# Whole-float32 units of a decayed-attention kernel: heads in pairs, states kept in a PSUM bank, a two-slot pool for the rest

## The chip, the cores and the metric

The kernel runs on one core of a Trainium2 chip. The metric is the device time of one execution in microseconds (us), the median over runs of the kernel. The core has five engines that run side by side and meet at semaphores: TensorE (PE; its weight loads are listed apart as PEld), VectorE (DVE), ScalarE (ACT), GpSimd (POOL) and SyncE (SP), which here only starts transfers.

## What is computed

A decayed linear attention over 4 batches, 8 heads, 768 steps and a head width of 64, in float32, and behind it a two-layer network with a softplus, whose weights come as float64:

```python
def _attn_ref(q, k, v):
    ...
    for t in range(S):
        state = gamma[None, :, None, None] * state + np.einsum('bhd,bhe->bhde', k[:, :, t], v[:, :, t])
        y[:, :, t] = scale * np.einsum('bhd,bhde->bhe', q[:, :, t], state)
    return y.astype(np.float32)

def _moe_ref(x, w_in, w_out):        # w_in 512x2048, w_out 2048x512
    h = x @ w_in
    g = np.maximum(h, 0.0) + np.log1p(np.exp(-np.abs(h)))
    return (g @ w_out).astype(np.float32)
```

Here x is the attention's output with the heads side by side: 3072 tokens of 512 values.

## The kernel before

**Units.** The sequence is cut into chunks of 128 steps. A unit is one chunk of one batch and one half (`hf`) of the heads, four heads: 4 batches x 6 chunks x 2 halves, 48 units; unit 2c + hf is chunk c of batch 0. The decay is folded into q and v by two tables on POOL (L134, L135), so that the state is a plain sum of k-by-v products. The steps of a unit are functions that the table `PARTS` places on ticks, four ticks to a unit: `load_unit`, `decay`, `operands` (PE transposes k and q two heads at a time into `tp`, ACT and DVE copy them out), `scores` (k by q into `sc`, copied to `ah`, the upper triangle cut away by POOL), `new_state` (k by v into `pp`), and `stack_and_outputs` (the chunk's output `yp` from the scores and the state of the chunk before, L255 to L266; then the next state `st`, L231 to L241).

**Two kinds of units.** The first 12 units (`WHOLE`, batch 0) feed float32 operands to PE. An fp32 product stands in the trace as two matmul records, two passes. The 36 others split every operand into a high and a low part of type float32r, each a product of one pass, and sum three products.

**A whole unit before.** A head's scores are taken with both heads' k of a pair as weights (`kw`, 128 columns) and the head's q between zeros (`qw`). States and outputs go head by head, with 64 weight columns: four `pp` products (L208), added by DVE into `td` in SBUF (L216, L219), copied to `st` by ACT (L231, L232), and an output of 64 partitions for each head, from state and q (L255) and from v and scores (L261). ACT and DVE write the output's high and low parts into the ring `xh`, `xl` in two pieces each (L270, L272).

**A split unit before.** Per head one product of the high k with v's high and low part side by side (L212, 64 columns of weights, 128 moving) and one of the low k with v's high part (L213, 64 by 64); two additions on DVE (L219, L221); then `st` as high and low part (L237 to L241).

**The network** (called FFN below) goes block by block over the tokens (`BLOCKS`: two of 256, six of 384, one of 256). A step has `hidden` (into `hp`, L300 to L302, 256 or 384 columns moving), a softplus over DVE, ACT and POOL (L307 to L316) and `second` (into `acc`, L331 to L333, 512 columns). Its weights come in 16 slices `f`. `convert_weights` turns the float64 bits of a slice into a high and a low float32r part: ACT L84 and L90, DVE L92 to L94, ACT L96 (high part), POOL L97 (low part), through one PSUM buffer `wp`. A slice's load waits until the slice three before it has been converted (`FETCH`). Slices 0 to 9 are first used by block 0, 10 to 15 by block 1.

**Order.** A scheduler sets each engine's order from the code's order and from dependencies; each engine then runs its list in order. PSUM has eight banks: two for `hp`, three for `acc` and `wp`, and three slots of pool `ps_a`, taken in turn by `tp`, `sc`, `pp` and `yp`; a new tile waits until the tile three allocations back has been read.

## Time and profile before

| | before |
|---|---|
| three timed runs | 698.87, 698.94, 699.02 us |
| median | 698.94 us |
| the profiled execution's span | 699.0 us |
| busy: PE, DVE, ACT, POOL | 683.4, 444.5, 366.1, 284.0 us |
| read from HBM, written | 35.66 MB, 6.29 MB |

The span runs from the first to the last instruction of one profiled execution; it is as long as the slowest of the timed runs to the digit shown, so nothing has to be added for what lies around it. Busy time of PE counts overlapping matmuls once. A matmul's own duration is longer than what it costs in a row of them, because they are pipelined: its cost is the distance from its start to the start of the next.

### The profile page before, as it was taken

The page shows a single profiled execution, that of the slowest core. Times are in us where ns is not written, and L with a number is a line of the kernel's source. Part 1 is how long each engine was busy: PE and PEld are TensorE (multiplying, and loading weights), DVE is VectorE, ACT ScalarE, POOL GpSimd, SP SyncE. Part 2 cuts the span into 40 slices and gives each one's busy share as a digit, 9 for nine tenths or more (in the row PEclk, how much of TensorE's full clock was granted, in tenths as well). Part 3 has the DMA queues.
Part 4 walks back from the last instruction along what each step waited for, and adds up shares of the span by engine and source line. Part 5 has one row for each costly group of instructions (what it writes and reads, how often), then busy time and mean ns, then how long its engine had stood idle before and what let it go on. Part 6 is the DMA issues. An engine that isn't in the chain of part 4 may idle for free.

```text
span 699.0 us, 12543 instructions
## 1 busy us (share of the span) xinstructions
PE 683.4 (98%) x4480; PEld 618.7 (89%) x4480; DVE 444.5 (64%) x940; ACT 366.1 (52%) x854; POOL 284.0 (41%) x346
## 2 busy tenths in 40 slices
PE   6699999999999999999999999999999999999997
PEld 5588888999999999999999999999999999999996
DVE  4786777576757776566776676567667666533321
ACT  4886776464555546455554654455565444433221
POOL 5675577443333433433343333334334332322221
PEclk9999999999999999999999999999999999999999
DMA  9975751221111121111211112111211101000100
GB/s 257 248 199 177 197 174 24 46 68 40 46 38 24 31 69 38 31 23 39 69 31 23 38 37 63 38 23 32 68 38 24 31 16 61 1 1 0 46 1 31
DMA packets 90750, 42.77 MB, mean 61 GB/s; under 512 B 77376, under 2 KB 85568, under 8 KB 90688
## 3 DMA queue, kind: packets, MB, share of 16 engines
q1 hardware_dynamic: 90240, 41.96, 22.1%
q8 instruction: 36, 0.59, 0.4%
q14 instruction: 26, 0.21, 0.1%
q10 hardware_dynamic: 448, 0.01, 0.0%
HBM read 35.66 MB, written 6.29 MB: 60 GB/s over the span
## 4 chain that ended last, share of the span: by engine, by line
PE 87%; DMA 1%; DVE 0%; ACT 0%; issue 0%
PE acc L331 13%; PE hp L300 12%; PE acc L333 12%; PE acc L332 12%; PE hp L302 12%; PE hp L301 12%; PE sc L188 2%; PE pp L212 1%; PE yp L266 1%; PE yp L264 1%; PE yp L265 1%; PE tp L142 1%; PE tp L144 1%; PE yp L258 1%; PE yp L257 1%; DMA win<-in_moe_w_in_dram 1%
## 5 line engine op out<-in xcount | busy, mean ns | idle before, releaser
L316 POOL TENSOR_TENSOR gl<-sp,gh 128x384 fp32r<-128x384 f32 (+1 forms) x120 | 130.1, 1084 | 201.6 <-ACT gh L314 151.0
L300 PE MATMUL hp<-xh,winhl 128*128 128x384 f32 (+1 forms) x576 | 186.5, 324 | 0.3 <-DVE sp L312 0.3
L302 PE MATMUL hp<-xh,winhl 128*128 128x384 f32 (+1 forms) x576 | 183.8, 319 | 0.0
L301 PE MATMUL hp<-xl,winhl 128*128 128x384 f32 (+1 forms) x576 | 183.6, 319 | 0.0
L331 PE MATMUL acc<-wouthl,gh 128*128 128x512 f32 x384 | 155.5, 405 | 0.0
L332 PE MATMUL acc<-wouthl,gh 128*128 128x512 f32 x384 | 150.7, 393 | 0.0
L333 PE MATMUL acc<-wouthl,gl 128*128 128x512 f32 x384 | 150.4, 394 | 0.0
L307 DVE TENSOR_SCALAR sp<-hp 128x384 uint32<-128x384 uint32 (+1 forms) x120 | 69.7, 582 | 98.0 <-PE hp L302 93.7
L308 ACT ACTIVATE sp<-sp 128x384 f32<-128x384 f32 (+1 forms) x120 | 65.6, 546 | 97.7 <-DVE sp L307 97.3
L300 PEld LDWEIGHTS hp<-xh,winhl 128*128 128x128 f32 x576 | 108.8, 189 | 4.9 <-issue 0.5
L301 PEld LDWEIGHTS hp<-xl,winhl 128*128 128x128 f32 x576 | 108.9, 189 | 3.6 <-DVE xl L272 0.2
L302 PEld LDWEIGHTS hp<-xh,winhl 128*128 128x128 f32 x576 | 108.7, 189 | 0.9 <-issue 0.5
L314 ACT CAST gh<-sp 128x384 fp32r<-128x384 f32 (+1 forms) x120 | 64.0, 534 | 78.7 <-DVE sp L312 44.4
L312 DVE SCALAR_TENSOR_TENSOR sp<-hp,sp 128x384 f32<-128x384 f32 (+1 forms) x120 | 69.5, 579 | 25.7 <-ACT sp L308 24.8
L333 PEld LDWEIGHTS acc<-wouthl,gl 128*128 128x128 f32 x384 | 71.9, 188 | 15.4 <-issue 0.2
L331 PEld LDWEIGHTS acc<-wouthl,gh 128*128 128x128 f32 x384 | 72.2, 188 | 11.2 <-issue 0.3
L332 PEld LDWEIGHTS acc<-wouthl,gh 128*128 128x128 f32 x384 | 72.4, 189 | 10.2
L159 DVE TENSOR_TENSOR kq<-tp,kq 64x256 fp32r<-64x256 f32 x72 | 30.4, 422 | 68.6 <-ACT kq L157 67.5
L134 POOL TENSOR_TENSOR qn<-qn,qtabs 128x256 f32<-128x256 f32 x48 | 29.4, 613 | 105.5 <-DMA qn<-in_q_dram 80.5
L156 ACT CAST kq<-tp 64x512 fp32r<-64x512 f32 x72 | 41.8, 581 | 29.4 <-PE tp L144 27.8
L135 POOL TENSOR_TENSOR vn<-vn,vtabs 128x256 f32<-128x256 f32 x48 | 29.4, 613 | 48.5 <-DVE al L191 18.5
L272 DVE TENSOR_TENSOR xl<-yp,xh 64x256 fp32r<-64x256 f32 x96 | 39.9, 416 | 5.5 <-ACT xh L270 4.2
(85 smaller groups left out, 1088.4 us busy)
## 6 DMA issues: line engine op xcount, KB each, us to landing
win<-in_moe_w_in_dram SPq DMA_DIRECT2D x16, 512.0 KB, 4.1
wout<-in_moe_w_out_dram SPq DMA_DIRECT2D x16, 512.0 KB, 4.1
kn<-in_k_dram SPq DMA_DIRECT2D x48, 128.0 KB, 2.4
qn<-in_q_dram SPq DMA_DIRECT2D x48, 128.0 KB, 2.7
vn<-in_v_dram SPq DMA_DIRECT2D x48, 128.0 KB, 2.3
out_dram<-o SPq DMA_DIRECT2D x24, 256.0 KB, 2.1
gtab_sb<-in_gtab_dram ACTq DMA_DIRECT2D x2, 2.0 KB, 3.3
qtabs<-in_qtab_dram ACTq DMA_DIRECT2D x1, 4.0 KB, 2.3
```

The source lines that it names most:

```text
L156: nc.scalar.copy(kq[own, :2, par], tp[own])
L300: nc.tensor.matmul(hp[:, k], lhsT=wt[:, 0, d, :], rhs=xh[:, d, :], start=d == 0, stop=False)
L301: nc.tensor.matmul(hp[:, k], lhsT=wt[:, 0, d, :], rhs=xl[:, d, :], start=False, stop=False)
L302: nc.tensor.matmul(hp[:, k], lhsT=wt[:, 1, d, :], rhs=xh[:, d, :], start=False, stop=d == ND - 1)
L307: nc.vector.tensor_scalar(sp.bitcast(U32), hps[s].bitcast(U32), 0x80000000, None, op0=ALU.bitwise_or)
L308: nc.scalar.activation(sp, sp, AF.Softplus)
L312: nc.vector.scalar_tensor_tensor(g, hps.pop(s), 0.0, g, op0=ALU.max, op1=ALU.add)
L314: nc.scalar.copy(gh, g)
L316: nc.gpsimd.tensor_tensor(gl, sps.pop(s), gh.bitcast(F32), op=ALU.subtract)
L331: nc.tensor.matmul(acc[i][t], lhsT=gh[:, k, ts], rhs=wt[:, 0], start=begins and k == 0, stop=False)
L332: nc.tensor.matmul(acc[i][t], lhsT=gh[:, k, ts], rhs=wt[:, 1], start=False, stop=False)
L333: nc.tensor.matmul(acc[i][t], lhsT=gl[:, k, ts], rhs=wt[:, 0], start=False, stop=ends and f == fs[-1])
```

## The change

The last unit kinds, numbers and names stay; lines move down by 10 or so (L300 becomes L310, L331 becomes L341).

- **States in PSUM.** A bank of its own, `stp`, holds the sums for both halves, two head pairs each. A product takes both heads' k of a pair as weights (128 columns) and both heads' v as moving columns (128). Of the 128x128 result the two 64x64 diagonal blocks are the states; the other two blocks hold mixed products that are never read. The sums run on over a batch's chunks, and the first product of a batch clears the bank. `td` and its additions are gone. A split unit's state takes six products (three for each pair) where it took eight, a whole unit's two where it took four.
- **Pool.** `ps_a` has two slots instead of three.
- **Whole units.** k stands between zeros (`kz`), q as it is (`qs`). The state sits in `stw`, zero off the diagonal blocks, v between zeros (`vns`, three buffers that also take the split units' v). An output is 128 partitions for a pair: one product from the state and two from the scores, each with 128 weight columns. ACT and DVE write `xh` and `xl` in one piece of 128 partitions.
- **Split units** copy the state from PSUM in two ACT copies and two DVE subtractions (`od` is gone); their scores and outputs are as before.
- **Setup.** DVE clears the zero halves of `vns` and `stw`, POOL those of `kz`.

How the rows of the engines' lists move, at three places. First PE, around the scores of unit 3, where the FFN begins; before (names: `st_231` is the state of half 1, `sc`, `pp`, `tp`, `yp` the PSUM tiles of the steps above):

```order
L180 MATMUL sc<-qw,kw 128x128 x4
L208 MATMUL pp<-vn,kn 64x64 x4
L300 MATMUL hp<-xh,winhl 128x256 x2
L142 MATMUL tp<-ident,kn 128x128 x2
L144 MATMUL tp<-ident,qn 128x128 x2
L255 MATMUL yp<-qw,st_231 64x128
L301 MATMUL hp<-xl,winhl 128x256
```

and of the change:

```order
L310 MATMUL hp<-xh,winhl 128x256
L187 MATMUL sc<-qs,kz 128x128 x4
L311 MATMUL hp<-xl,winhl 128x256
L312 MATMUL hp<-xh,winhl 128x256
L225 MATMUL stp<-vn_89,kn 128x128 x2
```

The state's four 64x64 products became two of 128x128, and a first matmul of the FFN now stands ahead of unit 3's scores.

Second ACT, in the rows that lead up to the copies of unit 3's transposes (`tp_278` before, `tp_262` in the change), on which those scores wait; before (`winhl_394` and `wp_398` belong to slice 2, `win_268` is slice 3 as loaded):

```order
L96 CAST wouthl_334<-w_330 128x512
L84 ACTIVATE win_268<-win_268 128x512
L96 CAST winhl_394<-w_390 128x512
L90 ACTIVATE wp_398<-wout_203 128x512
L148 COPY kw_283<-tp_278 128x256
L149 COPY qw_83<-tp_278 64x256
```

and of the change (`winhl_360` is slice 2):

```order
L97 CAST wouthl_311<-w_307 128x512
L157 COPY kz_85<-tp_262 64x256
L264 CAST xh_81<-yp_270 128x2x128
L85 ACTIVATE win_256<-win_256 128x512
L159 COPY qs_86<-tp_262 128x256
L241 COPY stw0_87<-stp_92 64x2x64
L97 CAST winhl_360<-w_356 128x512
```

Slice 2's cast and the `wp` row stood ahead of the unit's copies; now they stand behind them.

Third PE, at the state of a split unit in the middle of the program; before (four such pairs of rows follow each other, two are shown, `acc_2126` is a result of the FFN's block):

```order
L332 MATMUL acc_2126<-wouthl,gh 128x512
L333 MATMUL acc_2126<-wouthl,gl 128x512
L212 MATMUL pp<-vhl,kh 64x128
L213 MATMUL pp<-vhl,kl 64x64
L212 MATMUL pp<-vhl,kh 64x128
```

and of the change, for a later unit:

```order
L312 MATMUL hp<-xh,winhl 128x384
L225 MATMUL stp<-vhl,kh 128x128 x2
L225 MATMUL stp<-vhl,kl 128x128
L195 MATMUL sc<-kq_83 128x256 x2
L225 MATMUL stp<-vhl,kh 128x128 x2
```

Eight products with 64 weight columns became six with 128.

The diff (in the split branch of `outputs`, and in the old copies to the ring, lines that only change their place are left out):

```diff
--- before.py
+++ after.py
@@ -49,7 +49,8 @@
     ffn = ctx.enter_context(tc.tile_pool(name="ffn", bufs=2))
     ps_h = ctx.enter_context(tc.tile_pool(name="ps_h", bufs=2, space=bass.MemoryType.PSUM))
     ps_o = ctx.enter_context(tc.tile_pool(name="ps_o", bufs=1, space=bass.MemoryType.PSUM))
-    ps_a = ctx.enter_context(tc.tile_pool(name="ps_a", bufs=3, space=bass.MemoryType.PSUM))
+    ps_a = ctx.enter_context(tc.tile_pool(name="ps_a", bufs=2, space=bass.MemoryType.PSUM))
+    ps_s = ctx.enter_context(tc.tile_pool(name="ps_s", bufs=1, space=bass.MemoryType.PSUM))
 
     nc.scalar.preload_act_table_set("softplus")
 
@@ -114,7 +115,16 @@
 
     kqs = [attn.tile([P, 3, 2, NJ, C], F32R, name=f"kq{i}") for i in range(2)]
 
-    qws = [attn.tile([P, 2, NJ, C], F32, name="qw", tag="vhl", bufs=2) for i in range(2)]
+
+
+    kz = attn.tile([P, 2, NJ, C], F32, name="kz", tag="vhl", bufs=2)
+    qs = attn.tile([P, 2, NJ, C], F32, name="qs", tag="vhl", bufs=2)
+    stw = [attn.tile([P, NJ, P], F32, name=f"stw{hf}", tag=f"st{hf}") for hf in range(2)]
+    vns = [attn.tile([P, HH, 2, D], F32, name=f"vn{i}") for i in range(3)]
+
+
+    stp = ps_s.tile([P, 2, NJ, P], F32, name="stp")
+    sides = ((0, lo, up), (1, up, lo))
 
     def load_unit(n):
         if n in loads:
@@ -122,7 +132,7 @@
         b, c, hf = units[n]
         tiles = []
         for nm, src in (("kn", k), ("qn", q), ("vn", v)):
-            t = attn.tile([P, HH, D], F32, name=nm, bufs=3 if nm == "vn" else 2)
+            t = vns[n % 3][:, :, 0, :] if nm == "vn" else attn.tile([P, HH, D], F32, name=nm, bufs=2)
             nc.sync.dma_start(t, src[b, hf * HH:(hf + 1) * HH, c * C:(c + 1) * C, :].rearrange("h s d -> s h d"))
             tiles.append(t)
         loads[n] = tiles
@@ -143,15 +153,13 @@
         for j in range(NJ):
             nc.tensor.transpose(tp[:, 1, j, :], qn[:, 2 * j:2 * j + 2, :], ident)
         if n < WHOLE:
-            kw = attn.tile([P, NJ, C], F32, name="kw", tag="kh")
-            qw = qws[n % 2]
-            nc.scalar.copy(kw, tp[:, 0])
-            nc.scalar.copy(qw[lo, 0], tp[lo, 1])
-            nc.vector.tensor_copy(qw[up, 1], tp[up, 1])
-            live[n] = [(kw, qw), kn, vn]
+            qt = qs[:, n % 2]
+            nc.scalar.copy(kz[lo, 0], tp[lo, 0])
+            nc.vector.tensor_copy(kz[up, 1], tp[up, 0])
+            nc.scalar.copy(qt, tp[:, 1])
+            live[n] = [qt, kn, vn]
             return
         kq = kqs[n % 2]
-        sides = ((0, lo, up), (1, up, lo))
         for par, own, oth in sides:
             nc.scalar.copy(kq[own, :2, par], tp[own])
             nc.scalar.copy(kq[oth, 1, par], tp[own, 1])
@@ -173,11 +181,10 @@
     def scores(n):
         kq = live[n][0]
         if n < WHOLE:
-            kw, qw = kq
             parts = [attn.tile([P, HH, C], F32, name="ah")]
             sc = ps_a.tile([P, HH, C], F32, name="sc", tag="a")
             for h in range(HH):
-                nc.tensor.matmul(sc[:, h, :], lhsT=kw[:, h // 2, :], rhs=qw[:, h % 2, h // 2, :], start=True, stop=True)
+                nc.tensor.matmul(sc[:, h, :], lhsT=kz[:, h % 2, h // 2, :], rhs=kq[:, h // 2, :], start=True, stop=True)
             nc.scalar.copy(parts[0], sc)
         else:
             parts = [attn.tile([P, HH, C], F32R, name=nm) for nm in ("ah", "al")]
@@ -196,80 +203,83 @@
             )
         live[n] += parts
 
+    began = {}
+
     def new_state(n):
         b, c, hf = units[n]
-        live[n].append(state[hf][0] if c else None)
+        live[n].append(state[hf] if c else None)
         if c == NC - 1:
             return
-        pp = ps_a.tile([D, HH, 2, D], F32, name="pp", tag="a")
+        for j in range(NJ):
+            hs = slice(2 * j, 2 * j + 2)
+            if n < WHOLE:
+                kn, vn = live[n][1:3]
+                products = [(kn, vn)]
+            else:
+                vhl, kh, kl = live[n][1:4]
+                vh, vl = (vhl[:, :, t, :] for t in range(2))
+                products = [(kh, vh), (kh, vl), (kl, vh)]
+            for i, (kk, vv) in enumerate(products):
+
+                first = c == 0 and hf == 0 and j == 0 and i == 0
+                m = nc.tensor.matmul(
+                    stp[:, hf, j, :], lhsT=kk[:, hs, :], rhs=vv[:, hs, :], start=first, stop=True, skip_group_check=True
+                )
+                if first:
+                    began[b] = m.ins
+                elif c == 0:
+                    tc.add_manual_dep(m.ins, began[b].name, mybir.DependencyInfo(mybir.DependencyClass.NoSync, mybir.DependencyReason.DATA), reason="the bank's first")
+
+    def stack_state(n):
+        b, c, hf = units[n]
+        if c == NC - 1:
+            return
+        own_of = [(par, own, oth, stp[own, hf, :, par * D:(par + 1) * D]) for par, own, oth in sides]
+        if n + 2 < WHOLE:
+            st = state[hf] = stw[hf]
+            for par, own, oth, s in own_of:
+                (nc.scalar.copy if par else nc.vector.tensor_copy)(st[own, :, par * D:(par + 1) * D], s)
+            return
+        st = state[hf] = attn.tile([P, 2, NJ, D], F32R, name=f"st{hf}", bufs=1)
+        for par, own, oth, s in own_of:
+            nc.scalar.copy(st[own, par], s)
+        for par, own, oth, s in own_of:
+            nc.vector.tensor_tensor(st[oth, par], s, st[own, par].bitcast(F32), op=ALU.subtract)
+
+    def outputs(n):
+        b, c, hf = units[n]
+        kq, *rest, st = live.pop(n)
+        off, g = places[n // 2], hf * NJ
+        xh, xl = (x[:, g:g + NJ, off:off + C] for x in xring)
         if n < WHOLE:
-            kn, vn = live[n][1:3]
-            for h in range(HH):
-                nc.tensor.matmul(pp[:, h, 0, :], lhsT=kn[:, h, :], rhs=vn[:, h, :], start=True, stop=True)
-        else:
-            vhl, kh, kl = live[n][1:4]
-            for h in range(HH):
-                nc.tensor.matmul(pp[:, h], lhsT=kh[:, h, :], rhs=vhl[:, h], start=True, stop=False)
-                nc.tensor.matmul(pp[:, h, 0, :], lhsT=kl[:, h, :], rhs=vhl[:, h, 0, :], start=False, stop=True)
-        if c == 0:
-            td = attn.tile([D, HH, D], F32, name=f"td{hf}")
-            nc.vector.tensor_copy(td, pp[:, :, 0, :])
-        else:
-            td = state[hf][1]
-            nc.vector.tensor_tensor(td, pp[:, :, 0, :], td, op=ALU.add)
-        if n >= WHOLE:
-            nc.vector.tensor_tensor(td, pp[:, :, 1, :], td, op=ALU.add)
-        state[hf] = [None, td]
-
-    def stack_state(n):
-        b, c, hf = units[n]
-        if c == NC - 1:
-            return
-        tdv = state[hf][1].rearrange("d (j p) e -> d p j e", p=2)
-        if n + 2 < WHOLE:
-            st = attn.tile([P, NJ, D], F32, name=f"st{hf}", bufs=1)
-            nc.scalar.copy(st[lo], tdv[:, 0])
-            nc.scalar.copy(st[up], tdv[:, 1])
-            state[hf][0] = st
-            return
-        st = attn.tile([P, 2, NJ, D], F32R, name=f"st{hf}", bufs=1)
-        od = attn.tile([D, NJ, D], F32R, name="od")
-        nc.scalar.copy(st[lo, 0], tdv[:, 0])
-        nc.scalar.copy(od, tdv[:, 1])
-        nc.scalar.copy(st[up, 1], tdv[:, 1])
-        nc.vector.tensor_tensor(st[up, 0], tdv[:, 0], st[lo, 0].bitcast(F32), op=ALU.subtract)
-        nc.vector.tensor_tensor(st[lo, 1], tdv[:, 1], od.bitcast(F32), op=ALU.subtract)
-        state[hf][0] = st
-
-    def outputs(n):
-        b, c, hf = units[n]
-        kq, *rest, st = live.pop(n)
-        xh, xl = xring
-        off = places[n // 2]
+            kn, vn, a = rest
+            yp = ps_a.tile([P, NJ, C], F32, name="yp", tag="a")
+            v0 = vns[n % 3].rearrange("p h t d -> p (h t) d")
+            for j in range(NJ):
+                if c:
+                    nc.tensor.matmul(yp[:, j], lhsT=st[:, j, :], rhs=kq[:, j, :], start=True, stop=False)
+                for par in range(2):
+                    at = 2 * (2 * j + par) - par
+                    nc.tensor.matmul(yp[:, j], lhsT=v0[:, at:at + 2, :], rhs=a[:, 2 * j + par, :], start=c == 0 and par == 0, stop=par == 1)
+            nc.scalar.copy(xh, yp)
+            nc.vector.tensor_tensor(xl, yp, xh.bitcast(F32), op=ALU.subtract)
+            return
         yp = ps_a.tile([D, 2, NJ, C], F32, name="yp", tag="a")
+        vhl, kh, kl, ah, al = rest
         for j in range(NJ):
             for par in range(2):
                 h = 2 * j + par
                 o = yp[:, par, j, :]
...
+                if c:
                     nc.tensor.matmul(o, lhsT=st[:, par, j, :], rhs=kq[:, 1, par, j, :], start=True, stop=False)
                     nc.tensor.matmul(o, lhsT=st[:, par, j, :], rhs=kq[:, 2, par, j, :], start=False, stop=False)
-                if n < WHOLE:
-                    kn, vn, a = rest
-                    nc.tensor.matmul(o, lhsT=vn[:, h, :], rhs=a[:, h, :], start=c == 0, stop=True)
-                else:
-                    vhl, kh, kl, ah, al = rest
-                    nc.tensor.matmul(o, lhsT=vhl[:, h, 0, :], rhs=ah[:, h, :], start=c == 0, stop=False)
-                    nc.tensor.matmul(o, lhsT=vhl[:, h, 0, :], rhs=al[:, h, :], start=False, stop=False)
-                    nc.tensor.matmul(o, lhsT=vhl[:, h, 1, :], rhs=ah[:, h, :], start=False, stop=True)
...
+        for par, own, oth in sides:
+            nc.scalar.copy(xh[own], yp[:, par])
+        for par, own, oth in sides:
+            nc.vector.tensor_tensor(xl[own], yp[:, par], xh[own].bitcast(F32), op=ALU.subtract)
 
     def stack_and_outputs(n):
         outputs(n)
@@ -379,12 +389,15 @@
     nc.scalar.dma_start(gtab_sb[lo, 0], gtab)
     nc.scalar.dma_start(gtab_sb[up, 0], gtab)
     make_identity(nc, ident)
-    for qw in qws:
-        nc.gpsimd.memset(qw[up, 0], 0.0)
-        nc.gpsimd.memset(qw[lo, 1], 0.0)
+    for par, own, oth in sides:
+        nc.gpsimd.memset(kz[oth, par], 0.0)
+    for vn in vns:
+        nc.vector.memset(vn[:, :, 1, :], 0.0)
+    for st in stw:
+        nc.vector.memset(st, 0.0)
     for kq in kqs:
-        nc.gpsimd.memset(kq[up, 2, 0].bitcast(F32), 0.0)
-        nc.gpsimd.memset(kq[lo, 2, 1].bitcast(F32), 0.0)
+        for par, own, oth in sides:
+            nc.gpsimd.memset(kq[oth, 2, par].bitcast(F32), 0.0)
     nc.vector.reciprocal(gtab_sb[:, 1], gtab_sb[:, 0])
     for c in range(1, NC):
         nc.vector.tensor_tensor(qtabs[:, c], qtabs[:, c - 1], gtab_sb[:, 0], op=ALU.mult)
```

More of the change, by code (lines that the diff above doesn't have):

```diff
@@ L253, in outputs @@
                 o = yp[:, par, j, :]
-                if c and n < WHOLE:
-                    nc.tensor.matmul(o, lhsT=st[:, j, :], rhs=kq[1][:, par, j, :], start=True, stop=False)
-                elif c:
+                if c:
                     nc.tensor.matmul(o, lhsT=st[:, par, j, :], rhs=kq[:, 1, par, j, :], start=True, stop=False)
                     nc.tensor.matmul(o, lhsT=st[:, par, j, :], rhs=kq[:, 2, par, j, :], start=False, stop=False)
-                if n < WHOLE:
-                    kn, vn, a = rest
-                    nc.tensor.matmul(o, lhsT=vn[:, h, :], rhs=a[:, h, :], start=c == 0, stop=True)
-                else:
-                    vhl, kh, kl, ah, al = rest
-                    nc.tensor.matmul(o, lhsT=vhl[:, h, 0, :], rhs=ah[:, h, :], start=c == 0, stop=False)
-                    nc.tensor.matmul(o, lhsT=vhl[:, h, 0, :], rhs=al[:, h, :], start=False, stop=False)
-                    nc.tensor.matmul(o, lhsT=vhl[:, h, 1, :], rhs=ah[:, h, :], start=False, stop=True)
-        g = hf * NJ
-        to = [(par, x[rows, g:g + NJ, off:off + C]) for x in (xh, xl) for par, rows in ((0, lo), (1, up))]
-        for par, hi in to[:2]:
-            nc.scalar.copy(hi, yp[:, par])
-        for (par, low), (_, hi) in zip(to[2:], to[:2]):
-            nc.vector.tensor_tensor(low, yp[:, par], hi.bitcast(F32), op=ALU.subtract)
+                nc.tensor.matmul(o, lhsT=vhl[:, h, 0, :], rhs=ah[:, h, :], start=c == 0, stop=False)
+                nc.tensor.matmul(o, lhsT=vhl[:, h, 0, :], rhs=al[:, h, :], start=False, stop=False)
+                nc.tensor.matmul(o, lhsT=vhl[:, h, 1, :], rhs=ah[:, h, :], start=False, stop=True)
+        for par, own, oth in sides:
+            nc.scalar.copy(xh[own], yp[:, par])
+        for par, own, oth in sides:
+            nc.vector.tensor_tensor(xl[own], yp[:, par], xh[own].bitcast(F32), op=ALU.subtract)
     def stack_and_outputs(n):
```

1 line of the change is left out of this document (added).

## Prediction

> **What bounds the kernel now.** I read the page's head and its chain of work first, then the waits of PE, then stretches of time, then single matmuls.
>
> ```profile
> span 699.0 us, 12543 instructions
> PE 683.4 (98%) x4480; PEld 618.7 (89%) x4480; DVE 444.5 (64%) x940; ACT 366.1 (52%) x854; POOL 284.0 (41%) x346
> PE 87%; DMA 1%; DVE 0%; ACT 0%; issue 0%
> 27.85:80.00 52.15, 52.00 (x373) 45.28 (x374) 39.24 (x69) 39.90 (x86) 33.98 (x37) 0.97 0.67 188
> 27.85 1.81 PE L180 MATMUL sc<-qw,kw 128*128 128x128 f32 x8 [3.67 <-ACT qw L149]
> ```
>
> The stretch lists its length, then busy time of PE, PEld, DVE, ACT, POOL, then granted clock and DMA. PE is the bound: from 27.85 us (unit 3's scores) it is busy without a gap, and the chain of work is PE. Before that it waits, last 3.67 us for a copy on ACT. So a change of PE's work after 27.85 us should count in full, unless PE runs into another engine. There is one place where it nearly does, in the timeline of all engines:
>
> ```profile
> 69.74 0.62 ACT L96 CAST winhl<-w 128x512 fp32r<-128x512 f32 x1 [1.40 <-DVE w L94]
> 70.41 0.38 PE L300 MATMUL hp<-xh,winhl 128*128 128x256 f32 x1
> ```
>
> The cast of weight slice 8 ends at 70.36, and the first matmul that reads that slice starts at 70.41, between two halves of a unit's output. So up to the first use of slice 9, the last of block 0, PE's supply of weights is only just in time: PE is full because attention work fills what the conversions leave. Block 1's slices come into use later, and nothing after this shows a wait for weights.
>
> **The change, split units.** A state block of 6 products replaces one of 8. Its cost now, from the timeline of PE and of the weight loads:
>
> ```profile
> 501.88 0.39 PE L332 MATMUL acc<-wouthl,gh 128*128 128x512 f32 x1
> 502.10 0.22 PE L212 MATMUL pp<-vhl,kh 128*64 128x128 f32 x1
> ...
> 502.55 0.48 PE L333 MATMUL acc<-wouthl,gl 128*128 128x512 f32 x1
> 502.86 0.34 PE L301 MATMUL hp<-xl,winhl 128*128 128x384 f32 x1
> 502.17 0.13 PEld L212 LDWEIGHTS pp<-vhl,kh 128*64 128x64 f32 x1
> 502.22 0.14 PEld L213 LDWEIGHTS pp<-vhl,kl 128*64 128x64 f32 x1
> 505.82 0.19 PEld L331 LDWEIGHTS acc<-wouthl,gh 128*128 128x128 f32 x1
> 505.93 0.19 PEld L332 LDWEIGHTS acc<-wouthl,gh 128*128 128x128 f32 x1
> ```
>
> From L332's start to L301's are 0.98 us; L332 and L333 would take 0.23 each alone (502.10 less 501.88, and the same for its twin), so the block costs 0.52. Why 0.52 for so few columns: loads of 64 weight columns follow each other at 0.055 us, where matmuls leave no room, and a load of 128 columns at 0.11. Where the moving columns are few, PE waits for the load. The new block has six loads of 128 columns and streams 128 columns behind each: 6 x 0.11 = 0.66. That is 0.14 more for each of 30 units (the 36 less the last chunk of three batches): **+4.3 us**. No such product (128 by 128 in float32r) stands in the trace; bounds are 0.06, the step of an output product with 64 weight columns and 128 moving (170.10 to 170.16, quoted under rival 3), which makes 0.36 and -4.7 us, and 0.12, the step of a hidden matmul with 256 columns (46.79 to 46.91, next fence), which makes 0.72 and +6 us. I take 0.11, since the load is the nearest row.
>
> The Trainium skill, "TensorE: Matmul & The Clock Gate", section "Weight-path perf modes", speaks for the lower bound: weights are loaded faster when there are 128 columns of a type that is not FP32. If float32r counted as such a type, the block would stream; the 0.11 us between two loads says that it does not.
>
> **Whole units.** Three pieces of the timeline of PE:
>
> ```profile
> 44.98 1.06 PE L180 MATMUL sc<-qw,kw 128*128 128x128 f32 x8
> 45.96 0.68 PE L208 MATMUL pp<-vn,kn 128*64 128x64 f32 x8
> 46.57 0.39 PE L300 MATMUL hp<-xh,winhl 128*128 128x256 f32 x1
> 46.79 0.28 PE L301 MATMUL hp<-xl,winhl 128*128 128x256 f32 x1
> 46.91 0.29 PE L302 MATMUL hp<-xh,winhl 128*128 128x256 f32 x1
> ...
> 49.25 0.38 PE L144 MATMUL tp<-ident,qn 128*128 128x128 f32 x2
> 49.56 0.43 PE L255 MATMUL yp<-qw,st 128*64 128x128 f32 x2
> 49.93 0.73 PE L333 MATMUL acc<-wouthl,gl 128*128 128x512 f32 x2
> 50.50 0.40 PE L331 MATMUL acc<-wouthl,gh 128*128 128x512 f32 x1
> ...
> 52.00 0.28 PE L301 MATMUL hp<-xl,winhl 128*128 128x256 f32 x1
> 52.21 0.43 PE L261 MATMUL yp<-ah,vn 128*64 128x128 f32 x2
> ...
> 54.11 0.28 PE L300 MATMUL hp<-xh,winhl 128*128 128x256 f32 x1
> 65.68 0.38 PE L180 MATMUL sc<-qw,kw 128*128 128x128 f32 x2
> 65.82 0.48 PE L331 MATMUL acc<-wouthl,gh 128*128 128x512 f32 x1
> 66.13 0.39 PE L332 MATMUL acc<-wouthl,gh 128*128 128x512 f32 x1
> ```
>
> Two fp32 passes with 128 weight columns cost 66.13 - 65.68 - 0.23 = 0.22, so 0.11 a pass; eight of them 0.89. Scores and state of one unit take 46.79 - 44.98 - 0.12 = 1.69 (0.12 is the 256-column matmul in between), so the 8 passes of the state cost 0.80. They are short themselves, but PE stands still for 0.1 to 0.2 us at the way into and out of fp32 products with 64 weight columns; the scores, with 128, have no such gap (65.68). New: 4 passes of 0.11, 0.45. That is -0.35 for 7 units (3 to 9) after 27.85 us: **-2.5 us**. An output costs 50.50 - 49.25 - 0.22 - 2 x 0.23 = 0.57 for its first two passes and 54.11 - 52.00 - 2 x 0.12 = 1.87 for the other 14 (two 256-column matmuls taken off), 2.44 with two sets of gaps; undivided it would be 16 x 0.11 + 0.35 = 2.1. New: 12 passes of 0.11, 1.34. Four or five of the nine (units 3 to 11) are divided, so I take -0.9 each: **-8.1 us**. Scores and transposes keep their passes. PE's work after unit 3's scores so falls by 10.6 and grows by 4.3: **-6.3 us**.
>
> **What of it reaches the end.** Most of the 10.6 lies before slice 9's first use, where PE is only just fed. Following the new order of PE with these costs, PE has 43.7 us of work from unit 3's scores to the first use of slice 9, before it had 49.5; what is left after that is 613.0 against 613.5. So the end moves by 0.5 us plus what slice 9's first use moves, and that hangs on the conversions as well as on PE. Their chain runs over DVE and ACT in turn, behind the units' copies. What the change takes from these engines:
>
> ```profile
> L272 DVE TENSOR_TENSOR xl<-yp,xh 64x256 fp32r<-64x256 f32 x96 | 39.9, 416 | 5.5 <-ACT xh L270 4.2
> L219 DVE TENSOR_TENSOR td<-pp,td 64x256 f32<-64x256 f32 x32 | 13.2, 411 | 4.0 <-PE pp L213 3.7
> L192 DVE TENSOR_TENSOR al<-sc,al 128x256 fp32r<-128x256 f32 x72 | 28.2, 412 | 0.0
> L270 ACT CAST xh<-yp 64x256 fp32r<-64x256 f32 x96 | 35.0, 364 | 8.9 <-PE yp L266 5.4 <-PE yp L261 2.4
> L231 ACT COPY st<-td 64x128 f32<-64x128 f32 x10 | 2.9, 293 | 4.8 <-DVE td L216 2.8 <-PE yp L255 2.0
> L135 POOL TENSOR_TENSOR vn<-vn,vtabs 128x256 f32<-128x256 f32 x48 | 29.4, 613 | 48.5 <-DVE al L191 18.5 <-DMA vn<-in_v_dram 18.3 <-ACT kh L169 5.8
> ```
>
> By DVE's rows a whole unit loses an addition (0.41) and one of two ring subtractions (0.42; 128 partitions cost as much as 64 by L192) and gains a state copy (about 0.3): -0.5. By ACT's it loses one ring copy (0.36) and one of two state copies (0.29): -0.65. Over the nine units that come ahead of slice 9 that is 4.7 and 5.9 us. I take **-4.5 us** for slice 9's first use, near DVE's figure: a chain that goes through both gains what its slower link gains, and both are busy for three quarters of that stretch (39.2 and 39.9 of 52.15 us). Bounds: 0, if the chain is held by loads and waits rather than by work; -7.8, if PE alone sets the pace (its 5.8, and 2 of the 3.67 us ahead of 27.85, because slice 2's cast and the `wp` row, 0.6 each by the cast's row at 69.74, and DVE's work ahead of them no longer stand before the copies that unit 3's scores wait for). Sum: -4.5 - 0.5 = -5.0; 698.94 - 5.0 = **693.9 us**. The span is 0.1 us above the median, and the sum is taken as a difference, so this does not matter.
>
> **Costed at nothing.** DVE's five memsets of the setup stand where DVE waits for the first transfers; uncovered, five writes of 256 columns at L192's 0.41 are 2.1 us. In the split units DVE and ACT lose two additions and one copy; neither ends a wait of PE there, so no gain. POOL's pass over v now strides over zeros: unseen, between nothing and as much again (0.6 us a unit, L135 above), on a POOL that is 41% busy. A state product now waits for the other half's copies, since the bank is one tile; in the new order at least 4.4 us of PE work lie between a split unit's outputs and the next state, and the state's last copy, L240 under rival 3, ends at 172.42, 2.0 us behind the outputs' end (170.38). In whole units only 1.1 to 4 us lie there; a wait of 0.5 us in each of seven is inside the range.
>
> **Rivals.**
> 1. *PE alone sets the pace.* The conversions come with it, because their loads stand on SP's queue behind loads that wait for PE. Then -7.8 - 0.5 = -8.3, 690.6 us. For it: DVE and ACT are busy at three quarters in that stretch. Against: the wait at 69.74, 1.40 us of ACT for DVE.
> 2. *The conversions do not move.* Then only 0.5 us is left: 698.4 us. For it: every slice from 5 to 9 was just in time. Against: the copies in their way shrink.
> 3. *The two-slot pool makes PE wait* (slower). A score tile of a split unit now takes the slot of the output before it, which must have been read. In the new order at least 4.7 us of PE work lie between them. The longest such reading took:
>
> ```profile
> 170.10 0.22 PE L265 MATMUL yp<-al,vhl 128*64 128x128 f32 x1
> 170.16 0.22 PE L266 MATMUL yp<-ah,vhl 128*64 128x128 f32 x1
> 172.14 0.28 DVE L240 TENSOR_TENSOR st<-td,st 64x128 fp32r<-64x128 f32 x1
> 173.66 0.84 DVE L272 TENSOR_TENSOR xl<-yp,xh 64x256 fp32r<-64x256 f32 x2
> ```
>
> It ends at 174.50, 4.1 us after the output's end at 170.38. So PE waits only if readings come later than that by over 0.6 us. At 0.2 us over all 36 units this is +7.2, 701.1 us.
> 4. *128-column loads are fast in this place*, so that the state block streams: -4.7 in place of +4.3, 684.9 us. The 0.11 us between loads is against it.
>
> **How the numbers follow.** Forecast 0.47 (691.5 to 697.5), rival 1 0.21 (688.5 to 691.5), rival 2 0.15 (697.5 to 700.3), rival 3 0.13, rival 4 0.04. The range leaves out rival 4, the low edge of rival 1 and rival 3: 689.3 to 700.5. A measurement of this kernel can tell 0.2%, 1.4 us, from no change. Faster by more: the forecast, rivals 1 and 4, and a little of 2, 0.74; within it 0.13; slower 0.13.
>
> **What would show it.** In the changed kernel's profile, L225 in split units should have weight loads 0.11 us apart and cost 0.66 a unit, 24 us in all with the whole units' passes; a unit's fp32 outputs 1.34 without gaps beside them. PE should have short waits for ACT L97 or DVE L322 between 25 and 75 us that were not there; if there are none and 690 comes out, rival 1 is right. Slice 9's first use should fall some 4.5 us earlier. Waits of PE on DVE L282 or ACT after 130 us would be rival 3. If unit 3's scores start no earlier than 27.85 us, or if gaps stay around fp32 products with 128 weight columns, the sum is wrong.

## The result and the profile after

| | before | after |
|---|---|---|
| timed runs, median | 698.9 us (698.66 to 699.02) | **691.4 us** (690.48 to 691.96) |
| ratio | | 0.9887, 95% interval 0.9872 to 0.9903 |
| the profiled execution's span | 699.0 us | 690.2 us |

The change takes 7.5 us; 5.0 were forecast. The spans differ by 8.8, 1.3 more than the medians: the timed runs of after have spans of 688.8 to 690.2 us, some 1.8 us below their times, so the profiled execution of before, with a span as long as its timed runs' times, was one of its slower ones.

The page's head for after, and the waits of PE (us in total, times, longest):

```profile
span 690.2 us, 12071 instructions
PE 675.2 (98%) x4340; PEld 618.9 (90%) x4340; DVE 417.0 (60%) x873; ACT 354.5 (51%) x802; POOL 283.0 (41%) x344
PE sc L187 <- ACT qs L159: 2.3, 5, 0.8
PE hp L310 <- ACT xh L264: 0.5, 1, 0.5
PE hp L312 <- POOL winhl L98: 0.4, 1, 0.4
```

PE's busy time falls by 8.2 us, and PE still is busy for 98%: the bound has not changed hands. DVE lost 27 us of work and ACT 12. The last two rows are waits that before did not have, one of them for a weight slice, and in this execution they are short. A second profiled execution of the change ("after, again" below, span 689.0 us) shows the wait for a slice at five times that, the longest wait of PE apart from the one for its first input. Its rows, the wait and the stretch from unit 3's scores to the first use of slice 9 (length, busy PE, PEld, DVE, ACT, POOL, granted clock, DMA):

```profile
62.92 0.39 PE L312 MATMUL hp<-xh,winhl 128*128 128x256 f32 x1 [2.02 <-POOL winhl L98]
23.38:70.16 46.78, 44.66 (x339) 41.91 (x340) 36.67 (x65) 38.43 (x78) 36.10 (x41) 1.00 0.85 245
```

Now the stretch from unit 3's scores to the first use of slice 9, from the timeline of PE and POOL, first of after (the low part of slice 9, ten passes of an output, then the slice's first matmul), then of before:

```profile
25.76 1.16 PE L187 MATMUL sc<-qs,kz 128*128 128x128 f32 x8 [0.45 <-ACT qs L159]
69.22 1.31 POOL L98 TENSOR_TENSOR winhl<-w,winhl 128x512 fp32r<-128x512 f32 x1
70.35 0.61 PE L263 MATMUL yp<-ah,vn 128*128 128x128 f32 x4
70.79 0.39 PE L260 MATMUL yp<-qs,stw 128*128 128x128 f32 x2
71.02 0.61 PE L263 MATMUL yp<-ah,vn 128*128 128x128 f32 x4
71.38 0.36 PE L310 MATMUL hp<-xh,winhl 128*128 128x256 f32 x1
```

```profile
78.68 1.31 POOL L97 TENSOR_TENSOR winhl<-w,winhl 128x512 fp32r<-128x512 f32 x1
79.44 0.36 PE L300 MATMUL hp<-xh,winhl 128*128 128x256 f32 x1
```

Slice 9 is ready, with its low part, at 70.5 instead of 80.0 and first used 8.1 us earlier (the first matmul reads the high part alone). The two stretches and what is left behind them, before first, then after:

```profile
27.85:79.44 51.59, 51.44 (x369) 44.77 (x370) 38.70 (x69) 39.90 (x86) 33.43 (x37) 0.97 0.67 188
79.44:699.00 619.56, 615.44 (x4018) 560.89 (x4016) 390.59 (x838) 309.82 (x733) 233.76 (x279) 1.00 0.16 41
```

```profile
25.76:71.38 45.62, 44.64 (x339) 41.90 (x340) 36.23 (x63) 38.19 (x78) 35.56 (x39) 1.00 0.81 234
71.38:690.20 618.82, 614.96 (x3923) 563.65 (x3921) 365.63 (x772) 301.82 (x695) 232.66 (x278) 1.00 0.15 41
```

The clock of 0.97 hides a stretch at half clock. Windows of 2 us show it, before first, then after:

```profile
24.00:28.00 4.00, 0.33 (x3) 0.15 (x2) 2.62 (x4) 2.99 (x7) 3.40 (x4) 1.00 0.87 267
28.00:30.00 2.00, 1.85 (x12) 1.44 (x13) 1.90 (x4) 1.61 (x5) 0.31 (x2) 0.76 0.91 273
30.00:32.00 2.00, 2.00 (x13) 1.74 (x11) 1.82 (x5) 1.67 (x4) 2.00 (x3) 0.50 0.74 176
32.00:34.00 2.00, 2.00 (x14) 1.52 (x12) 1.07 (x2) 1.57 (x4) 0.40 (x1) 0.89 0.86 248
```

```profile
20.00:22.00 2.00, 1.04 (x5) 1.08 (x6) 1.80 (x3) 1.48 (x4) 2.00 (x3) 0.69 1.14 292
22.00:24.00 2.00, 2.00 (x12) 2.00 (x11) 1.62 (x5) 0.53 (x2) 1.70 (x3) 0.50 1.05 304
```

In before PE stands for 3.67 us up to 27.85, starts, and about 1 us later runs at half clock. Summed over its windows, the clock takes 2 x (0.24 + 0.50 + 0.11) = 1.7 us from PE, all behind 27.85, where PE is the bound. In after the same loss falls before 26 us, where PE also waits for other engines.

So the 8.8 us between the two spans are: unit 3's scores 2.1 earlier; PE's work up to slice 9 at full clock 51.44 - 1.7 = 49.7 against 44.6, 5.1 less; 1.7 of half clock gone from that stretch; 0.8 more of PE standing in it (0.98 against 0.15); 0.7 less behind it. 2.1 + 5.1 + 1.7 - 0.8 + 0.7 = 8.8. In "after, again" unit 3's scores come 4.5 earlier than before, PE stands 2.1 us in the stretch instead of 0.15, and slice 9's first use, at 70.16, is 9.3 earlier.

### The profile page after: what moved, and what is told of

It is laid out like the page before. It is cut to its first block, busy times and chain, and to the rows that moved or that the text cites. A ratio compares the mean times of both kernels' runs of the same rounds, so it can differ in the third digit from the quotient of the medians.

```text
span 690.2 us, 12071 instructions
## 1 busy us (share of the span) xinstructions
PE 675.2 (98%) x4340; PEld 618.9 (90%) x4340; DVE 417.0 (60%) x873; ACT 354.5 (51%) x802; POOL 283.0 (41%) x344
## 4 chain that ended last, share of the span: by engine, by line
PE 94%; DMA 3%; ACT 1%; SPq 1%; POOL 1%; issue 0%; POOLq 0%
PE hp L310 13%; PE acc L341 13%; PE hp L312 13%; PE hp L311 13%; PE acc L343 13%; PE acc L342 13%; PE stp L225 3%; PE sc L195 3%; PE tp L154 1%; PE tp L152 1%; PE yp L278 1%; PE yp L277 1%; PE yp L276 1%; DMA kn<-in_k_dram 1%; PE yp L275 1%; PE yp L274 1%
## 5 line engine op out<-in xcount | busy, mean ns | idle before, releaser
L310 PE MATMUL hp<-xh,winhl 128*128 128x384 f32 (+1 forms) x576 | 185.9, 323 | 0.5 <-ACT xh L264 0.5
L341 PE MATMUL acc<-wouthl,gh 128*128 128x512 f32 x384 | 154.6, 403 | 0.0
L310 PEld LDWEIGHTS hp<-xh,winhl 128*128 128x128 f32 x576 | 108.8, 189 | 3.9 <-ACT xh L264 0.7
L341 PEld LDWEIGHTS acc<-wouthl,gh 128*128 128x128 f32 x384 | 72.3, 188 | 10.5
L201 POOL TENSOR_SCALAR_AFFINE_SELECT ah<-ah 128x512 fp32r<-128x512 f32 (+1 forms) x48 | 31.4, 654 | 33.3 <-DVE al L198 26.3
```

The lines of the kernel that those rows point to most:

```text
L310: nc.tensor.matmul(hp[:, k], lhsT=wt[:, 0, d, :], rhs=xh[:, d, :], start=d == 0, stop=False)
L341: nc.tensor.matmul(acc[i][t], lhsT=gh[:, k, ts], rhs=wt[:, 0], start=begins and k == 0, stop=False)
```

## The experiments

For all of them one table, from each page and from windows of 2 us: the span of the profiled execution, PE's busy time, what of it was lost at half clock, the remainder, which is PE's work at full clock, and the time in which PE was not busy.

| kernel | span | PE busy | lost at half clock | PE's work | PE not busy |
|---|---|---|---|---|---|
| before | 699.0 | 683.4 | 1.7 | 681.7 | 15.6 |
| after | 690.2 | 675.2 | 1.7 | 673.5 | 15.0 |
| after, again | 689.0 | 673.9 | 0 | 673.9 | 15.1 |
| split states by head | 687.1 | 672.3 | 1.7 | 670.6 | 14.8 |
| split states in pairs | 681.7 | 667.1 | 0 | 667.1 | 14.6 |
| split states in the bank alone | 700.5 | 686.4 | 1.7 | 684.7 | 14.1 |
| two slots alone | 697.1 | 681.3 | 0 | 681.3 | 15.8 |
| ring in halves | 695.9 | 677.3 | 3.4 | 673.9 | 18.6 |
| high part in halves | 697.1 | 678.0 | 3.4 | 674.6 | 19.1 |
| low part in halves | 694.1 | 675.9 | 1.7 | 674.2 | 18.2 |
| scores twice | 695.3 | 681.7 | 0 | 681.7 | 13.6 |
| whole states by head | 689.3 | 674.4 | 0 | 674.4 | 14.9 |
| whole outputs in halves | 693.6 | 673.9 | 1.7 | 672.2 | 19.7 |
| pairs and whole outputs | 686.5 | 667.5 | 1.7 | 665.8 | 19.0 |

PE's work depends on the kernel's products alone: where only copies were changed it stays between 673.5 and 674.6. The rest of a span is waiting and half clock. Ratios below are to before, with 95% intervals; by its time, a split-state kernel is compared with the change's 691.4 us and the later kernels with "after, again" (691.76 us, 690.95 to 695.92, ratio 0.9895, 0.9874 to 0.9916).

> The changed kernel itself on the same chip, as the mark for the others of this call. All theories: 691.4 us, 0.989 of before.

**Split states: two forms.** First the products of before, head by head, with the sums in SBUF again:

```diff
+        if n >= WHOLE:
+            for h in range(HH):
+                nc.tensor.matmul(pp[:, h], lhsT=kh[:, h, :], rhs=vhl[:, h], start=True, stop=False)
+                nc.tensor.matmul(pp[:, h, 0, :], lhsT=kl[:, h, :], rhs=vhl[:, h, 0, :], start=False, stop=True)
...
```

> The changed kernel, but the split units' states go head by head with 64 weight columns through SBUF sums as before the change (eight products, DVE additions); the whole units keep everything new. Theory 1 (the split state block's cost is set by 128-column weight loads, 0.67 us for six against 0.52 for eight, and PE sets the pace so that all of it counts): 30 x 0.15 = 4.5 us less than the changed kernel, 686.9 us. Rival (the state block is covered, or DVE's two more additions a unit take the gain back): 691.4 us or more.

688.28 us, ratio 0.9839 (0.9818 to 0.986): 3.1 us below the change, and 3.3 by PE's work, so the theory of the loads holds in its direction, at about 70% of its 4.5; where the other 1 us stays was not traced. Then both heads' k as weights, and both parts of v beside each other, 256 columns behind one load:

```diff
+            for j in range(NJ):
+                nc.tensor.matmul(pp[:, j], lhsT=kh[:, hs, :], rhs=vhl[:, hs], start=True, stop=False)
+                nc.tensor.matmul(pp[:, j, :, 0, :], lhsT=kl[:, hs, :], rhs=vhl[:, hs, 0, :], start=False, stop=True)
...
+            for par, own, oth in sides:
+                nc.vector.tensor_tensor(sums[hf][own], pp[own, :, par, 0, :], sums[hf][own], op=ALU.add)
+                nc.vector.tensor_tensor(sums[hf][own], pp[own, :, par, 1, :], sums[hf][own], op=ALU.add)
```

> The changed kernel, but a split unit's state takes two products a pair: the high k of both heads by the high and low v of both heads (256 moving columns, 0.12 us) and the low k by the high v (128 moving, 0.11 us), summed on DVE in four additions of 64 partitions. Theory 1: a block of 0.46 in place of 0.67, 30 x 0.21 = 6.2 us less than the changed kernel, 685.2 us. Rival (the DVE additions, 4 x 0.32 us a unit, become late for the next state or output): 687 us or more, with waits of PE on DVE in the profile.

684.76 us, ratio 0.9786 (0.9765 to 0.9807): the best version of the study, 6.6 us faster than the change. The block in the timeline of PE, in after, and two rows of the weight loads:

```profile
505.87 0.33 PE L312 MATMUL hp<-xh,winhl 128*128 128x384 f32 x1
506.04 0.33 PE L225 MATMUL stp<-vhl,kh 128*128 128x128 f32 x2
506.21 0.27 PE L225 MATMUL stp<-vhl,kl 128*128 128x128 f32 x1
506.32 0.39 PE L225 MATMUL stp<-vhl,kh 128*128 128x128 f32 x2
506.55 0.27 PE L225 MATMUL stp<-vhl,kl 128*128 128x128 f32 x1
506.66 0.45 PE L341 MATMUL acc<-wouthl,gh 128*128 128x512 f32 x1
506.94 0.40 PE L342 MATMUL acc<-wouthl,gh 128*128 128x512 f32 x1
506.15 0.19 PEld L225 LDWEIGHTS stp<-vhl,kl 128*128 128x128 f32 x1
506.26 0.30 PEld L225 LDWEIGHTS stp<-vhl,kh 128*128 128x128 f32 x2
```

and in the pairs:

```profile
511.58 0.39 PE L195 MATMUL sc<-kq 128*128 128x256 f32 x2
511.81 0.28 PE L218 MATMUL pp<-vhl,kh 128*128 128x256 f32 x1
511.92 0.22 PE L219 MATMUL pp<-vhl,kl 128*128 128x128 f32 x1
511.98 0.33 PE L218 MATMUL pp<-vhl,kh 128*128 128x256 f32 x1
512.15 0.22 PE L219 MATMUL pp<-vhl,kl 128*128 128x128 f32 x1
512.21 0.40 PE L321 MATMUL hp<-xh,winhl 128*128 128x384 f32 x1
512.44 0.34 PE L322 MATMUL hp<-xl,winhl 128*128 128x384 f32 x1
```

In after 506.94 - 505.87 less the neighbours' own 0.17 and 0.23 is 0.67, with the loads 0.11 apart; in the pairs 512.44 - 511.58 less 0.23 and 0.17 is 0.46, for the same columns behind four loads. Over the 30 units 30 x 0.21 = 6.3 of the 6.6 us. Weight loads are the price of the block.

**The split part and the pool alone**, on the kernel before:

```diff
-    ps_a = ctx.enter_context(tc.tile_pool(name="ps_a", bufs=3, space=bass.MemoryType.PSUM))
+    ps_a = ctx.enter_context(tc.tile_pool(name="ps_a", bufs=2, space=bass.MemoryType.PSUM))
+    ps_s = ctx.enter_context(tc.tile_pool(name="ps_s", bufs=1, space=bass.MemoryType.PSUM))
...
-        pp = ps_a.tile([D, HH, 2, D], F32, name="pp", tag="a")
+        pp = ps_s.tile([D, HH, 2, D], F32, name="pp", tag="s")
```

> The kernel before with the pool of PSUM slots cut from three to two and the state product in a bank of its own; nothing else. Theory: readings end before PE comes back to the slot, so within 0.7 us of 698.9. Rival (a score tile waits for the output's slot): 0.2 us a unit or more, over 706 us, with waits of PE on DVE before the scores.

> The kernel before, with only the split units' states kept in the PSUM bank with 128 weight columns (six products), and the two-slot pool; whole units as before. Theory 1: 30 x 0.15 = 4.5 us slower than before, 703.4 us. Rival (keeping sums in PSUM pays by itself, because two DVE additions and an ACT copy a unit are gone): 698.9 us or less.

The pool alone: 698.79 us, ratio 0.9989 (0.9978 to 1.0). With the split units' states in the bank as well: 702.14 us, ratio 1.0038 (1.0027 to 1.005). Two slots cost nothing; the bank costs split units 3.35 us, which PE's work shows too (684.7 against 681.3). So all of the gain, and some 11 us of it, comes from the whole units.

**What sets the pace of the whole units.** Theory 2 of these expectations was that PE alone does. Either PE's work was raised, or the one-piece copies were taken back with PE's work unchanged:

```diff
-            for h in range(HH):
+            for h in list(range(HH)) * (2 if n > 2 else 1):
                 nc.tensor.matmul(sc[:, h, :], lhsT=kz[:, h % 2, h // 2, :], rhs=kq[:, h // 2, :], start=True, stop=True)
```

> The changed kernel, but units 3 to 11 issue their score products twice into the same place: 8 more passes of 0.11 us a unit on PE, nothing more on the other engines. Theory 2: all of it counts and the conversions move back with PE: 9 x 0.89 = 8.0 us slower, 699.4 us, and the cast of slice 9 is later by about 6 us. Rival (the conversions set the pace up to slice 9): PE has slack there, the cast of slice 9 stays, and only the units behind it count, 2 to 3 x 0.89: 693.5 us.

```diff
-            nc.scalar.copy(xh, yp)
-            nc.vector.tensor_tensor(xl, yp, xh.bitcast(F32), op=ALU.subtract)
+            for par, own, oth in sides:
+                nc.scalar.copy(xh[own], yp[own])
+            for par, own, oth in sides:
+                nc.vector.tensor_tensor(xl[own], yp[own], xh[own].bitcast(F32), op=ALU.subtract)
```

> The changed kernel, but the whole units' outputs go into the ring in two pieces of 64 partitions again, so that DVE and ACT each do one more copy in each of the 12 units (0.42 and 0.36 us); PE's work is unchanged. Theory 2 (up to slice 9 PE sets the pace and the conversions follow it): within 1 us of the changed kernel, 690.5 to 692.5 us. Rival (the conversions moved forward because DVE and ACT were relieved, as the prediction took it): nine units of 0.4 us ahead of slice 9, 3.5 us slower, 695 us.

Scores twice: 697.04 us, ratio 0.9969 (0.9957 to 0.998), 5.3 us more. By the table 7.8 us of work came in and 1.5 of waiting went. The stretch from unit 3's scores to the first use of slice 9, to be read against 23.38:70.16 of "after, again":

```profile
23.61:69.89 46.28, 46.03 (x353) 43.68 (x354) 35.06 (x62) 36.64 (x75) 34.45 (x38) 1.00 0.81 232
```

Six of the nine units, 5.3 us of new passes, stand in it, and yet the slice's first use is 0.3 us earlier: the new order put 3.9 us of other products behind it, and PE stands 0.25 us instead of 2.1. Slice 9's cast on ACT ends 1.9 us later (68.14 against 66.21), where theory 2 had 6 and its rival 0. So the end of the kernel does not move with this mark alone when the order changes.

Ring in halves: 698.51 us, ratio 0.9989 (0.9976 to 1.0001), 6.8 us more, though PE's work is the same 673.9: 3.5 us of waiting and 3.4 at half clock. So theory 2 falls: PE's work counts, and with more copies the kernel is slower at the same PE work. The half clock in that run, in windows:

```profile
24.00:26.00 2.00, 0.95 (x6) 0.76 (x7) 1.74 (x5) 1.90 (x5) 0.81 (x2) 1.00 1.15 335
26.00:28.00 2.00, 2.00 (x13) 2.00 (x12) 1.02 (x2) 1.85 (x4) 1.61 (x2) 0.53 0.84 228
28.00:30.00 2.00, 2.00 (x13) 2.00 (x12) 1.20 (x3) 1.47 (x5) 1.21 (x3) 0.61 0.85 258
```

It follows a stretch in which PE was busy for half of the time. The next two take back one copy each: the `xh` loop alone, and the `xl` loop alone.

> The changed kernel with only the high part of a whole unit's output, written by ACT, in two pieces of 64 partitions; DVE's low part stays in one piece and PE's work is unchanged. Both pieces split cost 6.8 us (698.5 against 691.8). Theory 'sum': the conversions go through DVE and ACT in turn, so a copy more on either is added to the chain; ACT's copy is 0.36 us, nine units, 3.2 us: 695.0 us. Rival 'slower link', the prediction's rule: DVE sets the pace and ACT has room, so this one costs nearly nothing: 691.8 us, at most 692.5. Spells at half clock of 1.8 us each, which followed stops of PE in the first 30 us of some traces, can be added to either; PE's idle time and the granted clock are to be read with the time.

> The changed kernel with only the low part of a whole unit's output, written by DVE, in two pieces of 64 partitions; ACT's high part stays in one piece. Theory 'sum': DVE's copy is 0.42 us, nine units, 3.8 us: 695.6 us, and with the run before the two add up to the 6.8 us of both. Rival 'slower link': DVE is the slower one and carries nearly all of it: 697.5 to 698.5 us.

High part: 699.38 us, ratio 0.9996 (0.9985 to 1.0007), 7.6 us more. Low part: 694.84 us, ratio 0.9936 (0.9923 to 0.9949), 3.1 us more. The low part is where 'sum' put it, but neither theory holds for the pair: ACT's copy alone costs as much as both together (their intervals overlap), so they do not add up, and DVE is not the one that carries the cost. Half clock is not most of it: the two timed runs of the high part with mean clocks of 0.999 and 1.000 took 696.66 and 698.10 us, where those of "after, again" took 690.95 to 691.89. The table says what is alike: PE waits 3 to 4 us longer in each, and loses 1.7 or 3.4 at half clock. In the high-part kernel one of the two half-clock stretches lies at 40 us, between unit 3's scores and the first use of slice 9:

```profile
38.00:40.00 2.00, 0.85 (x5) 0.64 (x6) 1.97 (x6) 1.97 (x5) 1.28 (x1) 1.00 0.57 110
40.00:42.00 2.00, 2.00 (x12) 1.90 (x11) 1.93 (x4) 1.93 (x6) 1.79 (x2) 0.60 0.72 240
42.00:44.00 2.00, 2.00 (x10) 1.71 (x9) 0.76 (x2) 1.11 (x3) 2.00 (x3) 0.55 0.31 51
```

ACT and DVE are full (1.97 of 2.00 us each) while PE stands for more than half.

**Less work for PE.** First the whole units' state products head by head, as before the change, into the diagonal blocks:

```diff
+                for par, own, oth in sides:
+                    h = 2 * j + par
+                    m = nc.tensor.matmul(
+                        stp[own, hf, j, par * D:(par + 1) * D], lhsT=kn[:, h, :], rhs=vn[:, h, :], start=first, stop=True, skip_group_check=True
+                    )
...
```

> The changed kernel, but the whole units' state products go head by head with 64 weight columns, into the diagonal blocks of the same bank (the other blocks stay unwritten): four products of 64 by 64 in place of two of 128 by 128. Theory 3 (fp32 products with 64 weight columns have standing gaps at both ends of a block): the block costs 0.8 us in place of 0.45 and the kernel 7 x 0.35 = 2.5 us more, 693.9 us, with PE standing still for 0.1 to 0.2 us on both sides. Rival (the gaps came from the pool's slots or the sums on DVE, not from the shape): 8 passes of 0.055, no gaps, 691.4 us.

691.27 us, ratio 0.9883 (0.9867 to 0.9899): no different from the change. The rows show another reason than either theory had:

```profile
36.00 0.39 PE L354 MATMUL acc<-wouthl,gh 128*128 128x512 f32 x1
36.43 0.45 PE L226 MATMUL stp<-vn,kn 128*64 128x64 f32 x8
36.82 0.73 PE L355 MATMUL acc<-wouthl,gl 128*128 128x512 f32 x2
```

The 0.2 us ahead of them stays (0.43 from 36.00, where the 512-column matmul takes 0.23). But the eight passes and their exit take 0.39 where the prediction's fence shows 0.61 for before (45.96 to 46.57). What differs is where results go: the two heads of a pair now write different halves of the partitions, and their passes ran side by side. So outputs were tried in this form:

```diff
-                    nc.tensor.matmul(yp[:, j], lhsT=st[:, j, :], rhs=kq[:, j, :], start=True, stop=False)
...
+                    for par, own, oth in sides:
+                        nc.tensor.matmul(yp[own, j], lhsT=st[:, j, par * D:(par + 1) * D], rhs=kq[:, j, :], start=True, stop=False)
+                for par, own, oth in sides:
+                    nc.tensor.matmul(yp[own, j], lhsT=vn[:, h, :], rhs=a[:, h, :], start=c == 0, stop=True)
```

> The changed kernel with the outputs of whole units taken head by head with 64 weight columns, the two heads of a pair into the two halves of the partitions; copies, DVE, ACT and POOL as in the changed kernel. In the run with whole states by head such products went two at a time, 0.058 us for two, with 0.09 and 0.15 us of standing time at the ends: an output of 16 passes should take 8 x 0.06 + 0.24 = 0.7 us instead of 1.34, so 5.8 us less for PE in nine units. Theory 'PE sets the pace' (as the score products taken twice counted 6.3 of 8.0 in the profiled run): 4 to 5 us less, 687 us. Rival 'conversions set the pace as they stand now': PE waits for slices instead, and only what lies behind slice 9's first use is gained: 690.5 to 691.5 us, with over 4 us more of idle time on PE between 26 and 80 us.

> The same outputs of whole units on top of the best version so far (split states in pairs with v's two parts side by side, 684.8 us). 'PE sets the pace': 4 to 5 us less, 680 us. 'Conversions set the pace': 683.5 to 684.5 us.

The first, timeline of PE and its longest waits:

```profile
46.89 0.39 PE L260 MATMUL yp<-qs,stw 128*64 128x128 f32 x4
47.11 0.39 PE L263 MATMUL yp<-ah,vn 128*64 128x128 f32 x4
PE yp L260 <- ACT ah L188: 3.5, 2, 2.7
PE tp L152 <- ACT wout L85: 3.0, 1, 3.0
```

Four passes in 0.22 us, 0.055 each, half of the 0.11 of a pass alone; I had expected 0.03, from products with 64 moving columns, where these have 128. PE's work fell by 1.7 us, not 5.8. The time rose: 695.59 us, ratio 0.9935 (0.9913 to 0.9958), 3.8 us more than the change, and on top of the pairs 690.05 us, ratio 0.9857 (0.9842 to 0.9872), 5.3 us more than the pairs alone. Both theories said at least no loss. PE waits 4.6 us longer, and not for weight slices. The wait of 3.0 us, put down to L85, is for unit 3's k: its load lands at 20.70 us, and PE goes on at 20.84 (in after the same wait is 2.0). The wait of 2.7 us is for ACT's copy of a unit's scores (L188), which stands behind a conversion on ACT that waits for its own load:

```profile
77.96 0.66 ACT L85 ACTIVATE wout<-wout 128x512 f32<-128x512 f32 x1 [2.29 <-DMA wout<-in_moe_w_out_dram]
79.17 0.58 ACT L188 COPY ah<-sc 128x512 f32<-128x512 f32 x1
```

Part of the 3.8 us is half clock: the two timed runs of this kernel with a mean clock of 1.000 took 692.95 and 693.03 us, those of "after, again" 690.95 and 691.64, some 1.7 us less. The scheduler had set the order anew, as in each kernel of this part and the part before it: in whole outputs in halves, whole states by head and scores twice, whose ACT and DVE have the change's operations, 85 to 128 of the first 200 rows of ACT and of DVE hold another operation than in the change.

## Why the prediction was right, and where it was off

The time, 691.4, lies inside the range and on the forecast's side, but 2.5 us below 693.9. It falls 0.1 us into rival 1's stretch (688.5 to 691.5); the repeat, 691.76, falls into the forecast's. Some 0.9 of the 2.5 us is the split units' term, the rest lies in the whole units.

- **Split units, +4.3.** The block held: 0.67 where 0.66 was forecast, weight loads 0.11 apart, 0.15 x 30 = +4.5. The time took less: alone, by experiment, +3.35. Rival 4, the fast load of 128 columns, did not occur.
- **Whole units, -2.5 and -8.1.** The passes of after cost what was forecast: ten passes of an output take 1.03 us (70.35 to 71.38) without a gap at either end. In the first stretch PE's work fell by 5.1, forecast 5.8; behind it by 0.5, forecast 0.5.
- **Unit 3's scores** start 2.1 us earlier; the 2 us had been worked out, but were counted under rival 1 alone.
- **Two slots, and the state's wait for the other half's copies**, costed at nothing: held. The 3.9 us without PE behind slice 9's first use are the program's last stores, as before; PE has no waits in the split units, and the pool alone makes 0.9989. Rival 3 did not occur, nor did rival 2.
- **Slice 9's first use, -4.5: the term that was mis-sized.** It moved by 8.1. The step reads "a chain that goes through both gains what its slower link gains". That held back 3.3 of rival 1's 8.3 us as new waits of PE; the first trace shows 0.8 more standing in that stretch, "after, again" 2.0, nearly all of it a wait for a weight slice, the kind of sign that the prediction asked for. So what it held back was right in kind and too large. The conversions moved up by 9.5 us, more than the 4.7 of DVE or the 5.9 of ACT. And the rule itself is not borne out: the kernel with ACT's copies taken back is 7.6 us slower, with DVE's 3.1, with both 6.8, though each of them also has a new order.
- **What I did not see:** the clock of 0.97 stood in the first row that I quoted, and 0.03 of 52 us is 1.6 us; the working's 49.5 us of PE work for 51.6 us without a gap left it out. It followed the long stop ahead of unit 3's scores, and in after it falls ahead of the stretch. Over repeated runs this is smaller than the 1.7 us of one trace: the 23 runs of before that go with "after, again" have mean clocks of 0.994 to 0.998, none at 1.000; the 10 runs of after 0.993 to 1.000, three of them at 1.000.

The mechanism was right in this: the early stage is fed by conversions that share DVE and ACT with the units' copies, and the kernels with copies given back are 3 to 8 us slower at equal PE work, half clock included. Rival 1 comes nearer in size, but as a mechanism it falls with the same runs, and PE's 2.0 us wait for a slice in "after, again" speaks against it too. Nearest to all runs, as a reading and not shown, is a balance: more work on PE counts (scores twice, 5.3 of 7.8), less work on PE alone does not (whole outputs in halves), more work on the copies counts. The change took from both sides at once.

What stays open is how much of the 3 to 8 us is the copies' own time, how much the new order that the scheduler made of them, and how much half clock. Whole outputs in halves, with every copy as in the change, has slice 9 ready 3 us later than "after, again" (71.4 against 68.4 us), and whole states by head 3.3 us later (71.7), one with and one without a cost in time; but the change's own first trace has it at 70.5, 2.1 us later than its second with the same order, so single traces do not settle this. A run with the order held fixed was not tried.

## What to carry to other kernels

Where PE is full only because other work fills the gaps of its supply, count a change on both sides: what PE saves can be lost unless the copies and conversions that feed it come earlier too, and in whole outputs in halves, with a new order, the time rose although PE's work fell. In the split units, where PE waits for nothing, what PE saved counted in full (the pairs). Split a trace into PE's work at full clock, time at reduced clock and time not busy before comparing two kernels; the first follows from the products where their price has been seen (scores twice: 8.0 expected, 7.8 measured; whole outputs in halves, priced by a guess: 5.8 and 1.7), and the other two hold what a forecast misses. When a product has few moving columns its price is the weight load, so put more columns behind each load before saving products.
